# Sliding-window attention and a feed-forward pair on one core: dense 128-key segments in place of block-diagonal 64-key blocks

## The chip, the cores and the metric

The kernel runs on one core of a Trainium2 chip. The metric is the device time of one execution in microseconds (us). The engines are TensorE (PE in the profile, its weight loads PEld), VectorE (DVE), ScalarE (ACT), GpSimd (POOL) and SyncE (SP), which here only issues transfers. Each engine has its own queue of instructions and takes them in order; semaphores tie the queues together.

## What is computed

Eight batches of eight heads, 576 tokens, 64 elements a head. A query sees the keys at most 32 tokens away. The outputs of the heads, side by side, are the input of a feed-forward pair with a leaky ReLU between its layers. Inputs and output are 32-bit floats.

```python
B, H, S, D = q.shape                       # 8, 8, 576, 64
scores = (1 / sqrt(D)) * matmul(q, k.transpose(0, 1, 3, 2))
mask = abs(pos[:, None] - pos[None, :]) <= 32
attn = softmax(where(mask, scores, -1e9))
x = matmul(attn, v).transpose(0, 2, 1, 3).reshape(B * S, H * D)   # 4608 x 512
h = x @ w_in                               # 512 x 2048
out = maximum(0.01 * h, h) @ w_out         # 2048 x 512
```

## The kernel before

**Work units.** Heads go in pairs `p` (four pairs), batches in halves `hf` of 288 tokens. One attention *step* `i` is one pair in one half: 64 steps, `i // 8` the batch, `i // 4 % 2` the half, `i % 4` the pair (`where`, L267). Four steps fill the 288 columns of `xT` that one *group* `g` of the feed-forward needs: 16 `h` tiles of four matmuls each (`h_tile`, L360; matmul L348, ACT's leaky ReLU into `gT` L355), then output tiles `o` of 128 tokens, 16 matmuls each (`o_tile`, L381; L390, ACT's copy L395, SP's store L396), two or three to a group.

**Getting q and k transposed.** `load_qk` (L68) brings a pair's q and k into `qf`, `kf`. `cast_qk` (L186) makes them bf16 in `qb`, `kb`, which have a place for each of the four pairs. For batches 0 and 1 `transposes` (L218) turns them on TensorE and ACT copies them out. From batch 2 on (`BY_DMA = 2`) `transpose_dma` (L207) issues two transposing DMAs a pair on SP, one for q, one for k, and the rows come two tokens at a time (512 bytes), so that tokens lie even ones first. `place_keys` (L248) then has DVE copy the keys of the two heads into the two diagonal blocks of `kbd`: 64 keys of one head and 64 of the other in one 128 x 128 weight tile, zero elsewhere. `vbd` holds the values likewise (`cast_v`, L199). So one matmul serves both heads.

**A step.** `score(i)` (L270): five matmuls, one per 64-key block (`WIN`, L141), 544 columns in all, into `ps`; ACT's exponential into `e` (L280); POOL's product with the 0/1 mask into `prob` (L282). `join` (L287): DVE adds the two halves of `prob`. `sums` (L295): a matmul with block-diagonal ones (L301; two matmuls, L304, in the first twelve steps, which have no `join`) gives every row its head's sum in `s`, and DVE takes the reciprocal `r` (L309). `product` (L312): five matmuls with `vbd` into `x` (L320). `scaled` (L332): DVE writes `x * r` into `xT` (L334).

**Order.** The order on each engine is that of the program text (`manual_schedule`). `step()` (L420) runs: `join(i + 1)`, `score(i + 2)`, then `sums(i)`, `product(i)`, `scaled(i)`, then `place_keys`, then what is due in this step: casts and transposes for a pair of the next batch with the loads of the batch after it, or a cast of v and its next load. The transposes of batch `b` and pair `p` are due at step 8(b-1) + p + 2 (one earlier for batch 2), their placing at step 8(b-1) + 4 + p. The opening (L461 to L566: steps 0 to 8's score) is written out by hand: there `sums(i + 1)` stands ahead of `product(i + 1)`, so that a reciprocal runs early. After it a plan (L571 to L588) gives `h` tiles 0.49 us and quarter `o` tiles 0.86 us and spreads the steps between them; the last step of a group is due `LEAD = 4.0` us of the plan before the group's first `h` tile. `spend` (L592) runs what is due between tiles. `ps`, `s` and `x` have one buffer each, the `h` and `o` tiles four (`mmps`).

Of the kernel before, what the change touches and what calls it, by code (L numbers as in the profile page):

```python
# [16 lines left out]
def kernel(  # L17
# [9 lines left out]

    nc = tc.nc
# [8 lines left out]
    NB = S // 64  # L41
    HALF = S // 2
    DMC = DMODEL // 128
    FFC = DFF // 128
    EVEN = HALF // 2
# [5 lines left out]
    cast = ctx.enter_context(tc.tile_pool(name="cast", bufs=1))  # L51
    attn = ctx.enter_context(tc.tile_pool(name="attn", bufs=2))
    kt = ctx.enter_context(tc.tile_pool(name="kt", bufs=4))
    joined = ctx.enter_context(tc.tile_pool(name="joined", bufs=2))
    recip = ctx.enter_context(tc.tile_pool(name="recip", bufs=3))
# [6 lines left out]

    qf, kf, vf = {}, {}, {}
    RUN = S // 96

    BY_DMA = 2

    def load_qk(b, p, behind=None):  # L68

        for into, src, name in ((qf, q, "qf"), (kf, k, "kf")):
            t = fload.tile([96, 2, RUN * D], FP32, name=f"{name}{p}")
            if behind is not None:
                behind.memset(t[0:1, 0, 0:1], 0.0)
                behind = None
            heads = src[b, 2 * p:2 * p + 2]
            if b < BY_DMA:
                nc.sync.dma_start(out=t, in_=heads.rearrange("a (p c) d -> p a (c d)", c=RUN))  # L79
            else:  # L80
                nc.sync.dma_start(
                    out=t.rearrange("p a (g e) -> p a g e", g=3),
                    in_=heads.rearrange("a (g p c) d -> p a g (c d)", g=3, c=2),
                )
            into[b, p] = t

    def load_v(b, p):

        t = fload.tile([128, NB, D], FP32, name=f"vf{p}")
        for a in range(2):  # L90
            nc.sync.dma_start(  # L91
                out=t[64 * a:64 * a + 64],
                in_=v[b, 2 * p + a].rearrange("(c p) d -> p c d", p=64),
            )
        vf[b, p] = t
# [9 lines left out]

    ident_f = const.tile([128, 128], FP32)
# [4 lines left out]
    ones_bd = const.tile([128, 128], BF16)  # L111
    nc.vector.memset(ones_bd, 0.0)
    nc.vector.memset(ones_bd[0:64, 0:64], 1.0)
    nc.vector.memset(ones_bd[64:128, 64:128], 1.0)


    qb = const.tile([96, NPAIR, RUN, 2, D], BF16)
    kb = const.tile([96, NPAIR, RUN, 2, D], BF16)

    kbd = [const.tile([128, NPAIR, NB, 128], BF16, name=f"kbd{i}") for i in range(2)]  # L120
    vbd = [const.tile([128, NPAIR, NB, 128], BF16, name=f"vbd{i}") for i in range(2)]
    zero = const.tile([128, 1], BF16)
    nc.vector.memset(zero, 0.0)

    def clear(t, p):
        flat = t[:, p].rearrange("p n j -> p (n j)")
        nc.scalar.activation(
            out=flat, in_=zero.to_broadcast([128, NB * 128]), func=AF.Copy,
        )

    mask = [const.tile([128, 2, 2, EVEN], BF16, name=f"mask{i}") for i in range(2)]
    nc.vector.memset(mask[0][:, 1, :, 0:16], 0.0)
    nc.vector.memset(mask[1][:, 1, :, 128:EVEN], 0.0)
    nc.vector.memset(kbd[0], 0.0)
    clear(vbd[0], 0)
    clear(vbd[0], 1)
    clear(vbd[0], 2)

    WIN = [  # L141
        [((0, 0, 48), (2, 48, 64), (4, 112, 32)), ((1, 16, 64), (3, 80, 64))],
        [((4, 0, 32), (6, 32, 64), (8, 96, 48)), ((5, 0, 64), (7, 64, 64))],
    ]

    win = const.tile([128, 2, 3, 64], BF16)
    nc.gpsimd.memset(win, 1.0)
    for lo in (0, 64):
        w = win[lo:lo + 64]
        nc.gpsimd.affine_select(  # L150
            out=w, in_=w, compare_op=ALU.is_ge, fill=0.0,
            base=0, channel_multiplier=-1, pattern=[[1, 2], [0, 3], [2, 64]],
# [3 lines left out]
            base=2 * W, channel_multiplier=1, pattern=[[-1, 2], [0, 3], [-2, 64]],  # L156
        )
    nc.gpsimd.memset(vbd[0][:, 3], 0.0)
    win_f = win.rearrange("p c m i -> p c (m i)")

    def make_mask(hf):
        lo = (16, 32)[hf]
        nc.gpsimd.tensor_copy(out=mask[hf][:, 0], in_=win_f[:, :, lo:lo + EVEN])
        lo = (16, 0)[hf]
        nc.gpsimd.tensor_copy(out=mask[hf][:, 1, :, lo:lo + 128], in_=win_f[:, :, 0:128])

    NPROB = 6
    prob = const.tile([128, NPROB, 2, 2, EVEN], BF16)

    ps = scps.tile([128, 1024], FP32)  # L170
    P0 = 512 - HALF
    ps_v = ps[:, P0:P0 + 2 * HALF].rearrange("p (n c i) -> p n c i", n=2, c=2)
    nc.scalar.activation(
        out=ps[:, 512:512 + HALF], in_=zero.to_broadcast([128, HALF]), func=AF.Copy,
    )

# [7 lines left out]
    qT = {}  # L184

    def cast_qk(b, p, q_eng=None):  # L186
        for eng, src, dst in ((q_eng or nc.gpsimd, qf, qb), (nc.gpsimd, kf, kb)):
            if b < BY_DMA:
                parts = [(dst[:, p], src[b, p].rearrange("p a (c d) -> p c a d", d=D))]
            else:  # L190
                by_c = src[b, p].rearrange("p a (g c d) -> c p g a d", g=3, c=2)
                parts = [(dst[:, p, 3 * c:3 * c + 3], by_c[c]) for c in range(2)]
            for to, tok in parts:
# [142 lines left out]
    def weighted(i):  # L336
        if probs[i][2] is None:
            sums(i)
# [308 lines left out]
```

## Time and profile before

| what | value |
|---|---|
| runs | 318.67, 318.82, 319.0 us; median 318.82 us |
| profiled execution, its span | 318.5 us, 6474 instructions; the three runs lie 0.2 to 0.5 us above the span, and the page has no other time for this execution |
| granted TensorE clock | 1.000 |
| DMA | 49.46 MB in 108400 packets, mean 155 GB/s; SP's queue 66.8% of 16 engines, POOL's 8.0% |
| DMA landing, median | q 4.5, k 5.0, v 4.2, transposes 4.1 (q) and 3.2 us (k) |
| idle before POOL's mask | 87.8 us over 64 |

The span is cut into 40 slices of 8 us on the page; a digit is the busy share of an engine in a slice, in tenths. A row of the groups has the line, the engine, the operation, the tiles and shapes, the count, the busy time of the group, the mean length of one in ns, and the engine's idle time just before them with what ended it. The chain of waits is followed from the last instruction back to what released it; its pieces have start, length and work. `SPq` means the queue of SP: its rows are the issues of DMAs, and their length is the time that SP spends on issuing.

### The profile page before, as it was taken

To read this page: it belongs to the slowest core of one execution; us is meant where nothing else is said; L and a number is where in the kernel's file an instruction comes from. 1 tells how busy PE (TensorE), PEld (TensorE's weight loads), DVE (VectorE), ACT (ScalarE), POOL (GpSimd) and SP (SyncE) were. 2 spreads that over 40 slices of the span, in tenths; PEclk is the share of its full clock that TensorE was granted. 3 is DMA by queue.
4 is the path that set the end of the run, shared out by engine and by line. 5 is a ranking of instruction groups with operands and counts; after the bars stand their busy time and mean duration, and the time that the engine had idled before them with its cause. 6 is when DMAs were issued, how large, how long until landed. Compare 5 with 4: busy or idle time off the path is not lost.

```text
span 318.5 us, 6474 instructions
## 1 busy us (share of the span) xinstructions
PE 303.2 (95%) x2449; PEld 204.3 (64%) x2449; DVE 218.2 (69%) x259; ACT 182.6 (57%) x393; POOL 191.6 (60%) x251
## 2 busy tenths in 40 slices
PE   2679998999999999999999999999999999999996
PEld 1467774585765858576765858576665858576653
DVE  5678955869655997688755997688745988565100
ACT  7577698474652828374652828375552837464531
POOL 7798963974546866686546866586637866330000
PEclk9999999999999999999999999999999999999999
DMA  8999999997999995399735995399733430000101
GB/s 179 211 186 218 267 250 203 250 206 181 216 242 196 231 206 150 82 251 203 155 76 127 238 227 136 75 223 232 162 76 104 109 70 33 35 35 2 66 31 71
DMA packets 108400, 49.46 MB, mean 155 GB/s; under 512 B 68816, under 2 KB 103888, under 8 KB 108368
## 3 DMA queue, kind: packets, MB, share of 16 engines
q1 hardware_dynamic: 104144, 44.84, 66.8%
q0 software_dynamic: 4224, 4.19, 8.0%
q8 instruction: 19, 0.31, 0.4%
q14 instruction: 13, 0.11, 0.1%
HBM read 36.70 MB, written 9.44 MB: 145 GB/s over the span
## 4 chain that ended last, share of the span: by engine, by line
PE 89%; DMA 3%; DVE 2%; SPq 1%; POOL 1%; ACT 1%; issue 1%; DVEq 0%; ACTq 0%
PE mm L348 39%; PE mm L390 38%; PE x L320 5%; PE ps L275 4%; DMA kf<-in_k_dram 3%; PE s L301 2%; DVE r L309 2%; SPq L79 1%; POOL w_in_bf L448 1%; DVE xT L334 1%; PE tp L225 1%; PE s L304 1%; ACT vbd L203 0%; SPq L91 0%; POOL prob L282 0%
## 5 line engine op out<-in xcount | busy, mean ns | idle before, releaser
L309 DVE RECIPROCAL r<-s 128x288 f32<-128x288 f32 x64 | 125.2, 1956 | 56.5 <-PE s L301 53.3
L282 POOL TENSOR_TENSOR prob<-e,mask 128x576 bf16<-128x576 bf16 x64 | 81.5, 1274 | 87.8 <-ACT e L280 41.1
L348 PE MATMUL mm<-xT,w_in_bf 128*128 128x288 bf16 x1024 | 134.0, 286 | 0.3
L390 PE MATMUL mm<-w_out_bf,gT 128*128 128x512 bf16 (+2 forms) x592 | 130.4, 373 | 0.2 <-DMA w_out_bf<-in_moe_w_out_dram 0.2
L355 ACT ACTIVATE gT<-mm 128x288 bf16<-128x288 f32 x256 | 101.4, 412 | 24.8 <-PE mm L348 8.5
L348 PEld LDWEIGHTS <-w_in_bf 128*128 128x128 bf16 x1024 | 98.4, 98 | 24.8 <-issue 0.6
L390 PEld LDWEIGHTS <-gT 128*128 128x128 bf16 x592 | 56.3, 98 | 59.6 <-issue 0.3
L395 ACT ACTIVATE o_sb<-mm 128x512 f32<-128x512 f32 (+2 forms) x37 | 21.7, 586 | 92.0 <-PE mm L390 92.0
L280 ACT ACTIVATE e<-ps 128x576 bf16<-128x576 f32 x64 | 41.4, 648 | 9.4 <-PE ps L275 9.2
L197 POOL CAST kb<-kf 96x384 bf16<-96x384 f32 (+1 forms) x56 | 35.5, 656 | 4.6 <-DMA kf<-in_k_dram 4.6
L205 POOL CAST vbd<-vf 64x576 bf16<-64x576 f32 x50 | 34.5, 689 | 1.8 <-DMA vf<-in_v_dram 0.4
L334 DVE TENSOR_TENSOR xT<-x,r 128x288 bf16<-128x288 f32 x64 | 29.3, 458 | 8.2 <-PE x L320 1.2
L260 DVE COPY kbd<-kT 64x576 bf16<-64x576 bf16 x48 | 32.3, 672 | 0.3
L275 PE MATMUL ps<-qT,kbd 128*128 128x128 bf16 (+2 forms) x320 | 26.5, 215 | 1.8 <-DVE kbd L258 1.2
L275 PEld LDWEIGHTS <-kbd 128*128 128x128 bf16 x320 | 21.0, 100 | 10.6 <-DVE kbd L258 1.5
L320 PE MATMUL x<-prob,vbd 128*128 128x128 bf16 (+2 forms) x320 | 26.0, 213 | 1.3 <-ACT vbd L203 0.7
L197 POOL CAST qb<-qf 96x384 bf16<-96x384 f32 x48 | 24.5, 538 | 0.0
L320 PEld LDWEIGHTS <-vbd 128*128 128x128 bf16 x320 | 20.6, 99 | 3.9 <-ACT vbd L203 1.8
L292 DVE TENSOR_TENSOR both<-prob 128x288 bf16<-128x288 bf16 x52 | 19.7, 380 | 0.9
L301 PE MATMUL s<-both,ones_bd 128*128 128x288 bf16 x52 | 14.9, 286 | 0.0
L258 DVE COPY kbd<-kT 64x576 bf16<-64x576 bf16 x16 | 7.1, 444 | 8.7 <-ACT kT L239 8.6
L225 PE MATMUL tp<-ident,qb 96*128 96x96 bf16 x48 | 4.4, 243 | 6.2 <-DVE qb L197 6.2
(43 smaller groups left out, 86.6 us busy)
## 6 DMA issues: line engine op xcount, KB each, us to landing
qf<-in_q_dram SPq DMA_DIRECT2D x32, 288.0 KB, 4.5
kf<-in_k_dram SPq DMA_DIRECT2D x32, 288.0 KB, 5.0
vf<-in_v_dram SPq DMA_DIRECT2D x64, 144.0 KB, 4.2
out_dram<-o_sb SPq DMA_DIRECT2D x35, 256.0 KB, 3.6
w_in_bf<-in_moe_w_in_dram POOLq DMA_DIRECT2D x4, 512.0 KB, 8.6
w_out_bf<-in_moe_w_out_dram POOLq DMA_DIRECT2D x4, 512.0 KB, 16.8
qT<-qb SPq DMA_TRANSPOSE x24, 4.1
kT<-kb SPq DMA_TRANSPOSE x24, 3.2
```

Source lines behind the costliest of these rows:

```text
L197: eng.tensor_copy(out=to, in_=tok)
L205: nc.gpsimd.tensor_copy(out=vbd[b % 2][r, p, :, r], in_=vf[b, p][r])
L260: nc.vector.tensor_copy(out=to.rearrange("p n (m c) -> p n c m", c=2), in_=kT[r].rearrange("p (c n m) -> p n c m", c=2, n=NB),)
L275: nc.tensor.matmul(ps_v[:, n_, :, i0:i0 + n], kbd[b % 2][:, p, blk], by_c[:, :, hf * EVEN + i0:hf * EVEN + i0 + n], start=True, stop=True,)
L280: nc.scalar.activation(out=e, in_=ps[:, P0:P0 + 2 * HALF], func=AF.Exp, scale=scale)
L282: nc.gpsimd.tensor_mul(pr.rearrange("p n c i -> p (n c i)"), e, mask[hf].rearrange("p n c i -> p (n c i)"),)
L309: nc.vector.reciprocal(r, s)
L320: nc.tensor.matmul(x_v[:, :, i0:i0 + n], vbd[b % 2][:, p, blk, :], pr[:, n_, :, i0:i0 + n], start=(blk == parts[0][1]), stop=(blk == parts ...
L334: nc.vector.tensor_mul(place(i), x, r)
L348: nc.tensor.matmul(h[:, 0:HALF], w_in_bf[:, c, ts(f, 128)], xT[:, c, ds(g * HALF % RING, HALF)], start=(c == 0), stop=(c == DMC - 1),)
L355: nc.scalar.activation(out=gT[:, f, ds(g * HALF % RING, HALF)].rearrange("p (i c) -> p i c", c=2), in_=h[:, 0:HALF].rearrange("p (c i) -> ...
L390: nc.tensor.matmul(o[:, lo:hi], gT[:, f, ds(128 * j % RING, 128)], w_out_bf[:, f, lo:hi], start=(f == 0), stop=(f == FFC - 1),)
```

## The change

The block-diagonal tiles go. A weight tile for the scores is now 128 keys of *both* heads' transposed rows: 128 consecutive columns of `kT` (64 elements of each head on 128 partitions). The queries are kept twice, `qz[.., a, ..]` having the rows of head `a` and zeros in the other head's 64 partitions, so that the contraction over 128 partitions yields one head's scores. Eight segments of 128 keys, 64 apart (`SEG`), serve 96, 64, 64, 64 and again 64, 64, 64, 96 queries. For odd segments `kO` holds the two 64-key halves exchanged (`swap`, one copy a pair), so that each row of `v` serves both kinds of segment from the partition it was loaded into. The weight tile of the products is `[values of head 0 | ones | values of head 1]`, of which 128 columns are taken: for head 0 rows 0 to 63 of the result are weighted sums of values and rows 64 to 127 are row sums, for head 1 the other way round. So there are two results, `x0` and `x1` (one buffer each), no matmul for sums, no `join`; instead two copies bring the sums to the partitions of their head, and the reciprocal stands between product and multiply. Tokens keep their natural order.

What moves or changes in number, per pair or step:

- q and k loads from batch 2 on: four DMAs of 256-byte rows in place of two of 512-byte rows; v: three DMAs in place of two.
- transposing DMAs: three (q twice) in place of two, into buffers that stay for a batch; the bf16 sources have two places (`p % 2`) instead of four.
- casts: q on POOL is one instruction in place of two, and so is k; v three in place of two.
- DVE: `swap` (one copy) in place of two copies into `kbd`, due at the same step; two multiplies of 64 partitions in place of one of 128; one or two copies of sums (the other one on ACT).
- the opening is written anew; in it the masks of the first two steps are multiplied on DVE, the q casts of pairs 2 and 3 are on POOL, and the clearing on DVE is of `qz` and the ones in `vw`.
- `LEAD` is 5.0.

The diff, cut to its core:

```diff
     def load_qk(b, p, behind=None):
...
             else:
-                nc.sync.dma_start(
-                    out=t.rearrange("p a (g e) -> p a g e", g=3),
-                    in_=heads.rearrange("a (g p c) d -> p a g (c d)", g=3, c=2),
-                )
+                for a in range(2):
+                    nc.sync.dma_start(out=t[:, a], in_=heads[a].rearrange("(g p) d -> p g d", p=96))
...
     def load_v(b, p):
...
+        t = fload.tile([128, 2, 5, D], FP32, name=f"vf{p}")
         for a in range(2):
             nc.sync.dma_start(
+                out=t[:, a, 0:4], in_=v[b, 2 * p + a, 0:512].rearrange("(j p) d -> p j d", p=128),
             )
+        nc.sync.dma_start(
+            out=t[0:64, :, 4], in_=v[b, 2 * p:2 * p + 2, 512:S].rearrange("a p d -> p a d"),
+        )
...
+    zero_halves(nc.vector, 0)
+    nc.vector.memset(vw[0][:, :, :, 1], 1.0)
...
+    def cast_v(b, p, engs=None):
...
+        copy(e0, to[:, 0], src[:, 0:4])
+        copy(e1, to[0:64, 1], src[0:64, 1:5])
+        copy(e2, to[64:128, 1], src[64:128, 0:4])
...
     def transpose_dma(b, p):
+        for a in range(2):
+            nc.sync.dma_start_transpose(
+                out=qz[b % 2][:, p, a].rearrange("p (c i) -> p c i", c=RUN),
+                in_=qbz[p % NQZ][:, a].rearrange("p c a d -> p (c a d)"),
+            )
+        nc.sync.dma_start_transpose(
+            out=kT[b % 2][:, p].rearrange("p (c i) -> p c i", c=RUN),
+            in_=kb[:, p % NQB].rearrange("p c a d -> p (c a d)"),
+        )
+        landing.append((8 * (b - 1) + 4 + p, b, p))
...
+    def transposes(b, p, engs):
...
+            if which == "q":
+                for a in range(2):
+                    r = slice(64 * a, 64 * a + 64)
+                    copy(engs[a], qz[b % 2][r, p, a].rearrange("p (i c) -> p i c", c=RUN), tok[r])
             else:
+                copy(engs[2], kT[b % 2][:, p].rearrange("p (i c) -> p i c", c=RUN), tok)
+                swap(b, p, engs[3])
...
+    def score(i, mask_eng=None):
         b, hf, p = where(i)
+        for n in range(hf * HSEG, (hf + 1) * HSEG):
...
+            nc.tensor.matmul(
+                ps[:, P0[hf] + c0:P0[hf] + c1].rearrange("p (a i) -> p a i", a=2), kk,
+                qz[b % 2][:, p, :, SEG[n][0]:SEG[n][1]], start=True, stop=True,
+            )
...
+    def product(i):
...
+        for a in range(2):
+            for n in range(hf * HSEG, (hf + 1) * HSEG):
...
                 nc.tensor.matmul(
+                    x[a][:, SEG[n][0] - first:SEG[n][1] - first],
+                    vw[b % 2][:, p, n, a:a + 2].rearrange("p c d -> p (c d)"),
+                    pr[:, c0 + a * w:c0 + (a + 1) * w],
+                    start=True, stop=True,
                 )
...
+    def normalize(i, engs):
...
+        copy(engs[0], s[0:64], x[0][64:128])
+        copy(engs[1], s[64:128], x[1][0:64])
         r = recip.tile([128, HALF], FP32, name="r")
         nc.vector.reciprocal(r, s)
+        for a in range(2):
+            rows = slice(64 * a, 64 * a + 64)
+            nc.vector.tensor_mul(xT[rows, p, t0:t0 + HALF], x[a][rows], r[rows])
...
+    def step(engs, swap_eng):
         i = state["done"]
-        if JOINED - 1 <= i < NC - 1:
-            join(i + 1)
         if i < NC - 2:
             score(i + 2)
-        weighted(i)
-        place_keys()
+        product(i)
+        normalize(i, engs)
+        while landing and landing[0][0] <= i:
+            swap(*landing.pop(0)[1:], swap_eng)
...
+    cast_qk(0, 0, DVE)
+    make_mask(0, DVE)
+    transposes(0, 0, (ACT, ACT, ACT, DVE))
+    score(0, DVE)
+    cast_qk(0, 1, DVE)
+    transposes(0, 1, (ACT, ACT, ACT, DVE))
+    cast_v(0, 0)
+    score(1, DVE)
     product(0)
+    normalize(0, (ACT, ACT))
+    cast_qk(0, 2, POOL)
+    transposes(0, 2, (ACT, ACT, ACT, DVE))
+    keep_busy(ps, 768, 4)
+    score(2)
+    cast_qk(0, 3, POOL)
     load_w_in(0, 512)
+    keep_busy(ps, 768, 4)
+    cast_v(0, 1)
+    product(1)
+    normalize(1, (ACT, ACT))
     load_w_in(512, 1024)
+    transposes(0, 3, (ACT, ACT, ACT, DVE))
+    keep_busy(ps, 768, 8)
+    score(3)
     load_w_in(1024, 1536)
+    cast_v(0, 2, (POOL, ACT, ACT))
+    make_mask(1, POOL)
     h0 = h_first(0)
     h = next(h0)
+    product(2)
+    normalize(2, (ACT, ACT))
     keep_busy(h, HALF, 8)
+    score(4)
+    load_w_in(1536, 2048)
+    cast_v(0, 3, (POOL, ACT, ACT))
+    next(h0)
+    next(h0)
+    product(3)
+    normalize(3, (ACT, ACT))
...
     def second_half():
-
         i = state["done"]
-        weighted(i)
-        if i < 7:
-            sums(i + 1)
+        product(i)
+        normalize(i, (ACT, DVE))
         if i < 5:
             score(i + 3)
         state["done"] += 1
...
-    H_US, O_US, LEAD = 4 * (HALF / 2400 + 2.5e-3), 4 * 0.216, 4.0
+    H_US, O_US, LEAD = 4 * (HALF / 2400 + 2.5e-3), 4 * 0.216, 5.0
...
-            step()
+            step((DVE, DVE) if kind == "h" else (ACT, DVE), DVE)
```

## The prediction

> **What bounds the kernel now.** I read the busy shares, the chain of waits, the groups, then the timelines of SP and of the opening. From the page:
>
> ```profile
> PE 303.2 (95%) x2449; PEld 204.3 (64%) x2449; DVE 218.2 (69%) x259; ACT 182.6 (57%) x393; POOL 191.6 (60%) x251
> PE   2679998999999999999999999999999999999996
> PE 89%; DMA 3%; DVE 2%; SPq 1%; POOL 1%; ACT 1%; issue 1%; DVEq 0%; ACTq 0%
> ```
>
> TensorE is busy in all slices but the first few: its work is the time, and any wait placed before one of its matmuls is added to it. Its steady stretch, in the chain of waits (start, length, work):
>
> ```profile
> 191.88 3.43 PE mm L348 x28
> 195.31 0.24 PE ps L275 x5
> 195.55 0.12 PE s L301
> 195.68 0.24 PE x L320 x5
> 195.91 3.92 PE mm L348 x32
> ...
> 204.38 0.24 PE ps L275 x5
> ...
> 208.43 0.24 PE ps L275 x5
> ```
>
> An attention step costs 0.24 + 0.12 + 0.24 = 0.60 us of TensorE; steps stand 4.05 to 4.5 us apart, 17.15 us to a group of four. The other engines have only to keep this beat. How near they are to it:
>
> ```profile
> L309 DVE RECIPROCAL r<-s 128x288 f32<-128x288 f32 x64 | 125.2, 1956 | 56.5 <-PE s L301 53.3
> L334 DVE TENSOR_TENSOR xT<-x,r 128x288 bf16<-128x288 f32 x64 | 29.3, 458 | 8.2 <-PE x L320 1.2
> 131.10 1.25 SPq L212 DMA_TRANSPOSE qT<-qb  x1
> 132.44 1.20 SPq L212 DMA_TRANSPOSE kT<-kb  x1
> 133.70 0.57 SPq L81 DMA_DIRECT2D qf<-in_q_dram  x1
> 134.33 0.50 SPq L81 DMA_DIRECT2D kf<-in_k_dram  x1
> 134.92 0.45 SPq L396 DMA_DIRECT2D out_dram<-o_sb  x1
> 135.86 1.30 SPq L212 DMA_TRANSPOSE qT<-qb  x1
> ```
>
> (Two rows of the groups, six of SP's timeline.) SP spends 4.3 us of each step of this kind on issuing; the beat is 4.3.
>
> **TensorE's work.** Per matmul: 3.92/32 = 122.5 ns for 288 columns, 3.45/16 = 215.6 for 512, so 0.416 ns a column and 2.7 ns each; five of 544 columns make 0.240, as the rows show. New: four score matmuls with 576 columns 0.251, eight products with 576 columns 0.262, no sum: 0.51 us. Saved: 0.09 x 52 steps = 4.7 us; the first 12 steps lose a second sum matmul as well, but lie where TensorE will wait. Products of 64 columns at 29 ns each have a weight load per matmul; the old streams have one every 47 ns on average without a gap, which is the nearest row. Bounds: 29 ns holds (saving 4.7), or 47 ns is a floor (eight products 0.38: step 0.63, a loss of 1.6). I take 29.
>
> The Trainium skill, "TensorE: Matmul & The Clock Gate", section "Back-to-back issue gap", speaks against small matmuls: it gives some 81 ns for each 128-column matmul with its weight load; by it twelve instead of eleven would cost 0.08 us a step more. These rows deny it: five of 64 to 128 columns take 0.24 us, 48 each.
>
> **The opening** (the first four steps). Each engine runs in order, so I walk the compiled order with the row durations. DVE first clears two halves of qz and sets the ones: 4352 elements at 0.86 ns (the 2304-word memset took 1.98), 3.7 us against 2.4 of memsets now; its q cast starts at 5.65 (before 4.65). A pair then costs: q cast 1.0; 0.69 to ACT's first copy; three ACT copies (two halves of q, k) 0.60 apart, the last 0.65; swap 0.44 (L258's row); 0.75 from score to exponential; exponential 0.65; mask on DVE 0.6 (between 0.38, the 288-column add, and POOL's 1.27): 6.1. And DVE's q cast of pair 1 is queued *behind* mask 0, so pair 1's mask ends at 17.8. Then reciprocal 0 (1.96) and two 64-partition multiplies (0.46 each, starts 0.37 apart) to 20.7; swap 2 is queued behind them; score 2, exponential to 22.5; POOL's mask 2 (1.27) to 23.8, and *behind it* both casts of pair 3 (2 x 1.0), a w_in issue (0.8) and three v casts of pair 1 (0.6 each, from the 64x576 row of 0.69): 28.2. Only there can product 1 run. Two ACT copies of the sums, reciprocal, multiplies 32.2; swap 3, score 3, mask 3 35.3; w_in, v cast: product 2 at 36.8. Mask for half 1, mask 4, w_in, v cast: product 3 at 41.4; its normalization ends 45.5. So the fourth chunk of the first hidden tiles starts at 45.5, not where the chain has it now:
>
> ```profile
> 25.88 0.47 DVE xT L334
> 26.39 0.65 PE mm L348 x4
> 64.33 1.47 PE mm L348 x12
> ```
>
> That is **+19.2 us**. DMA no longer gates it: the last k load lands at 15.5. Bounds: a third of the links at half price, +12; TensorE running cold in its gaps (its six opening transposes take 0.66, later 0.42), +23.
>
> **Steps 4 to 7.** Old: s and x are separate, the reciprocal runs before the product, and a step waits 0.46 for one multiply. New: x0 and x1 have one buffer each and hold from product to multiply: 0.3 drain, copy 0.41, reciprocal 1.96, multiplies 0.83, some 0.1 at each of four handovers, ACT's queue of gT (0.41 each) and exponentials ahead of the copy: 3.7 to 4.4 us. The program gives 16 matmuls (1.96 us) between these steps. Walked: products at 47.3, 51.9, 55.8, 59.6 and group 1's fourth chunk done at 64.3, that is 17.0 us from product 4; now 28.15 to 36.95, 8.8. **+8.2** (6 to 10).
>
> **Steps 8 to 11** stand 12, 12 and 8 output matmuls apart (2.59, 2.59, 1.73 us plus 0.51). With four chains of 4.45 they take 17.8, now 51.06 to 64.33, 13.3; ahead of them some 1.9 of old waits go. **+2.6** (0 to 4).
>
> **The steady steps, x held.** Gaps from product to product become 3.95 or 4.45 us. x1 is free 4.07 us after the product with both copies on DVE, 4.2 to 4.4 with one on ACT behind the exponential and an o_sb copy (0.60), and is wanted at gap + 0.13. So a stall of 0 to 0.35 in half the steps: 0.25 a group, **+3** (0 to 8). DVE loses the add (0.38) and two key copies a pair (2 x 0.67) and gains copies, a second multiply and the swap: 3.3 to 3.7 a step plus 0.44 in half of them, against 4.2 (now 3.5 on average). No cover is left, so whatever DVE waits for stops TensorE.
>
> **SP's queue, and what waits for it.** Per pair of batches 3 to 6, SP now issues three transposes (1.30 from start to start, 3.9), four q/k loads with as many pieces each as the old two (0.59, 2.35) and 0.3 of output: 6.55 us, at a step of 4.2. The lag grows by 2.35 a pair, 7.05 at the fourth. Step start T; its casts end T+3.4; the fourth pair's k transpose is issued at 3.45 + 3 x 6.55 + 2.6 = 25.7 and lands 3.2 later, 28.9 (landing times 2.5 to 4.9). Its swap, an instruction of DVE, stands at T + 5 x 4.2 + 4.3 = 25.3; behind it on DVE are the next step's copies, reciprocal and multiplies, for which the next product's x waits. 3.6 us late a batch, four batches 14.4; batch 3 inherits up to 3 from batch 2 (whose transposes share SP with the v loads), and the x stalls give back about 1 a batch: **+14**. Bounds: 0, if the issues of 256-byte rows cost half; 22, if landing takes the 4.9 of the slowest. Batches 2 and 7 are in time: an extra step, or no loads. POOL's q cast is one instruction for two; its v casts three for two, +0.4 a step in half the steps, hidden by its idle time, 87.8 us over 64 masks; were it not, the mask still has two steps of lead. ACT's contiguous gT costs nothing either way: its strided rows of 288 and the plain ones of 512 columns (0.41, 0.59) lie on one line per column.
>
> **Sum**: 318.5 (span) - 4.7 + 19.2 + 8.2 + 2.6 + 3 + 14 = 360.8. The median of the three runs, 318.82, lies 0.3 above the profiled span: **361 us**.
>
> **Rivals.**
> A (0.57): the above, 351 to 373.
> B (0.20): SP is not late, since a swap finds its keys landed; the stalls of opening and x stay: 361 - 14 = 347, 342 to 351. For it: SP now idles up to 1.7 us a pair for POOL's casts. Against: the fourth burst's transpose follows the loads without a gap.
> C (0.09): the opening overlaps more than I walk, +10 instead of +19 and the groups behind it half: 318.8 - 4.7 + 10 + 5.4 + 3 + 3 = 335, 325 to 342.
> D (0.05), faster: TensorE's own work decides. If x is free before the next product, everywhere less than the gap (the chain under 2.5 us in group 0, that is, no reciprocal in it), the saved matmuls remain: 318.8 - 4.7 - 1.5 = 312.6. The 89% of the chain speaks for it; the reciprocal of 1.96 between product and multiply against.
> E (0.08): over 373: SP's lag carries over from batch to batch (4 x 6.55 and 4 x 1.9 for three v loads a pair, 33.8 us of issue, against 33.6 of beat) and loads come late too: 380.
> That it does nothing: 0.01; the order of every engine differs.
>
> The range leaves out D, E and the lower half of C: 334 to 373. The likeliest case's own range is 351 to 373. A change under 0.2% could not be told from none: faster 0.05, same 0.01, slower 0.94.
>
> **What would show it.** In the profile after: first slices of TensorE at 2 to 5 tenths until about 60 us; the h matmuls of the fourth chunk first starting near 45; product matmuls (x) idle before, released by DVE's multiply; DVE's swap idle before, released by the DMA of kT, in the last two pairs of batches 3 to 6; SP nearly without idle in those batches. Wrong if product 1 runs before 22 us, if SP's q/k issues take under 0.4 us, or if steady steps stand at 4.2 us throughout.

## The result and the profile after

The changed kernel takes **373.47 us** (median of four runs, 372.72 to 374.59) against 318.91 us for the kernel before in the same session (318.67 to 319.82): a ratio of 1.171, with a 95% interval of 1.168 to 1.173. Its profiled execution has a span of 372.2 us, 53.7 more than the 318.5 of before. The forecast was 361 us, with a range up to 373, so the measured time lies just above the range: direction and places are as walked, the size is 12.5 us short. In two experiments below one of four runs is a slow one, at a lower granted clock (358.62 us in loads later without the reciprocal, 370.13 us in both edits with the v loads on ACT); the medians given hold it, the ratios leave it out.

Of the page after, the busy shares, TensorE's slices (9.3 us each), the granted clock in the same slices, and the chain that ended last:

```profile
PE 314.0 (84%) x2504; PEld 205.2 (55%) x2504; DVE 249.5 (67%) x335; ACT 195.2 (52%) x427; POOL 194.7 (52%) x243
PE   1513686987999997689996999879998999999996
PEclk9999997899999999899999899989999999999999
PE 56%; DVE 16%; DMA 10%; POOL 6%; issue 6%; ACT 4%; SPq 2%; POOLq 0%; DVEq 0%; ACTq 0%
```

TensorE's first six slices stand at 1 to 8 tenths, and its row of nines is now broken in several later places. The chain is 56% TensorE where it was 89%; what came in is DVE (16%) and DMA (10%).

The two groups of DVE that were shown of before (work, shapes, count, then busy time and mean ns, then idle time and what ended most of it):

```profile
L287 DVE RECIPROCAL r<-s 128x288 f32<-128x288 f32 x64 | 125.0, 1953 | 27.0 <-ACT s L180 25.0
L290 DVE TENSOR_TENSOR xT<-x,r 64x288 bf16<-64x288 f32 x128 | 58.3, 455 | 4.5
```

The reciprocal costs what it did, but its idle time halved (56.5 to 27.0) and now ends with ACT's copy of the sums, no longer with a matmul; the multiplies doubled in number at almost the same length (455 ns, 458 before). In all DVE is busy for 249.5 us, 218.2 before.

The opening, in the chain of waits (start, length, work):

```profile
28.49 0.35 PE x L271 x3
...
29.73 1.96 DVE r L287
...
37.15 0.66 PE x L271 x8
...
42.74 0.43 PE x L271 x4
...
65.49 0.47 DVE xT L290
65.96 0.04 issue
66.00 1.12 PE mm L298 x4
```

Products 1, 2 and 3 stand within 1.4 us of where the prediction's walk through the queues put them (28.2, 36.8, 41.4), each behind POOL's v cast; product 1 is followed by two sums, the reciprocal and two multiplies. The last row is the fourth chunk of group 1, behind DVE's multiply; it ends near 66.5, before near 36.95.

SP in batch 3 (start, length, what is issued):

```profile
129.58 1.05 SPq L78 DMA_DIRECT2D vf<-in_v_dram  x2
130.68 0.61 SPq L81 DMA_DIRECT2D vf<-in_v_dram  x1
131.38 1.10 SPq L78 DMA_DIRECT2D vf<-in_v_dram  x2
132.53 0.61 SPq L81 DMA_DIRECT2D vf<-in_v_dram  x1
133.24 2.54 SPq L203 DMA_TRANSPOSE qz<-qbz  x2
135.88 1.22 SPq L207 DMA_TRANSPOSE kT<-kb  x1
137.15 1.14 SPq L71 DMA_DIRECT2D qf<-in_q_dram  x2
138.33 1.05 SPq L71 DMA_DIRECT2D kf<-in_k_dram  x2
139.48 0.52 SPq L340 DMA_DIRECT2D out_dram<-o_sb  x1
140.10 2.56 SPq L203 DMA_TRANSPOSE qz<-qbz  x2
```

SP has no pause beyond the 0.05 to 0.1 us between issues. From pair to pair (133.24 to 140.10) SP needs 6.86 us, where a step should take 4.2 to 4.5. The first transposes of the batch stand behind v loads, although their casts are done at 127.5; the last of them in POOL's rows:

```profile
126.64 0.83 POOL L182 CAST kb<-kf 96x768 bf16<-96x768 f32 x1
```

DVE some us later, in its timeline (start, length, work; in brackets idle time before it and what ended it):

```profile
146.28 2.54 DVE L182 COPY kO<-kT 128x512 bf16<-128x512 bf16 x1 [3.68 <-DMA kT<-kb]
148.75 0.93 DVE L182 COPY s<-x 64x288 f32<-64x288 f32 x2
149.72 1.95 DVE L287 RECIPROCAL r<-s 128x288 f32<-128x288 f32 x1
151.70 0.94 DVE L290 TENSOR_TENSOR xT<-x,r 64x288 bf16<-64x288 f32 x2
```

The waits of the whole span in which this shows (total us, times, longest):

```profile
DVE kO L182 <- DMA kT<-kb: 20.3, 10, 4.4
PE x L271 <- POOL vw L182: 15.6, 6, 3.8
PE x L271 <- DVE xT L290: 13.9, 12, 3.1
```

Four of the six waits put down to POOL's v cast (10.0 us) are those of the opening. The other two, 2.82 and 2.77 us ahead of products 33 and 41, are late swaps as well: the first ends at 202.89, when POOL's cast had been done since 199.27; DVE's first multiply, which frees x0, ends at 202.75.

And TensorE's timeline after it:

```profile
152.30 0.82 PE L271 MATMUL x<-prob,vw 128*128 128x64 bf16 x8 [3.08 <-DVE xT L290]
152.92 5.01 PE L334 MATMUL mm<-w_out_bf,gT 128*128 128x512 bf16 x16
```

Together they are the whole chain of a late swap: the copy kO waits 3.68 us for kT; behind it on DVE are the sums, the reciprocal and the multiplies; the next product stands 3.08 us, because x is still held. After the wait, 16 output matmuls took 5.01 us, and the granted clock was 0.50 from 152.4 to 155.7. The timeline of before has 3.62 for 16:

```profile
187.67 3.62 PE L390 MATMUL mm<-w_out_bf,gT 128*128 128x512 bf16 x16
```

**Where the 53.7 us of span are.** Up to the first h matmul of group 2 the kernel lost 32.7 us (97.02 against 64.33); from there to the end it took 275.2 us instead of 254.2, 21.0 more. For the second part I sorted TensorE's time by the distance from each matmul's start to the next: 0.416 ns a column and 2.7 ns is the work, a large excess is a gap, a small one a slow matmul. Work fell from 251.2 to 245.9; gaps rose from 0 to 20.9; slow matmuls from 0 to 5.3. Of the gaps, 17.3 us stand at the steps with a late swap, most of the rest comes 0.27 us at a time, x held.

### The profile page after: what moved, and what is told of

Same layout as the page of the kernel before. It is cut to its first block, busy times and chain, and to the rows that moved or that the text cites. A ratio compares the mean times of both kernels' runs of the same rounds, so it can differ in the third digit from the quotient of the medians.

```text
span 372.2 us, 6882 instructions
## 1 busy us (share of the span) xinstructions
PE 314.0 (84%) x2504; PEld 205.2 (55%) x2504; DVE 249.5 (67%) x335; ACT 195.2 (52%) x427; POOL 194.7 (52%) x243
## 4 chain that ended last, share of the span: by engine, by line
PE 56%; DVE 16%; DMA 10%; POOL 6%; issue 6%; ACT 4%; SPq 2%; POOLq 0%; DVEq 0%; ACTq 0%
PE mm L298 27%; PE mm L334 21%; DVE r L287 8%; PE x L271 4%; DVE xT L290 4%; DMA kT<-kb 3%; DMA vf<-in_v_dram 3%; PE ps L252 3%; DMA qf<-in_q_dram 2%; POOL prob L259 2%; DVE s L182 2%; POOL vw L182 2%; SPq L203 1%; ACT s L180 1%; DMA qz<-qbz 1%
## 5 line engine op out<-in xcount | busy, mean ns | idle before, releaser
L257 ACT ACTIVATE e<-ps 128x576 bf16<-128x576 f32 x64 | 41.6, 650 | 63.6 <-PE ps L252 59.0
L290 DVE TENSOR_TENSOR xT<-x,r 64x288 bf16<-64x288 f32 x128 | 58.3, 455 | 4.5
L271 PE MATMUL x<-prob,vw 128*128 128x64 bf16 (+1 forms) x512 | 33.7, 202 | 32.1 <-POOL vw L182 15.6
L182 DVE COPY s<-x 64x288 f32<-64x288 f32 x87 | 39.4, 453 | 31.9 <-PE x L271 30.3
L182 POOL CAST vw<-vf 64x512 bf16<-64x512 f32 (+1 forms) x88 | 52.4, 612 | 2.3 <-DMA vf<-in_v_dram 0.4
L271 PEld LDWEIGHTS <-vw 128*128 128x128 bf16 x512 | 24.8, 100 | 39.9 <-POOL vw L182 17.1
L182 POOL CAST kb<-kf 96x768 bf16<-96x768 f32 x32 | 27.8, 870 | 11.4 <-issue 6.4
L182 DVE COPY kO<-kT 128x512 bf16<-128x512 bf16 x32 | 14.2, 444 | 24.5 <-DMA kT<-kb 20.3
L252 PE MATMUL ps<-qz,kT 128*128 128x128 bf16 (+1 forms) x128 | 24.0, 236 | 5.6 <-ACT kT L180 5.6
L180 ACT ACTIVATE s<-x 64x288 f32<-64x288 f32 x41 | 16.7, 407 | 21.7 <-PE x L271 20.9
L252 PE MATMUL ps<-qz,kO 128*128 128x128 bf16 (+1 forms) x128 | 23.4, 236 | 4.2 <-DVE kO L182 4.1
L182 POOL CAST qbz<-qf 96x768 bf16<-96x768 f32 x24 | 19.6, 818 | 7.0 <-DMA qz<-qbz 7.0
```

The costliest lines, as they stand in the source:

```text
L180: eng.activation(out=to, in_=frm, func=AF.Copy)
L182: eng.tensor_copy(out=to, in_=frm)
L252: nc.tensor.matmul(ps[:, P0[hf] + c0:P0[hf] + c1].rearrange("p (a i) -> p a i", a=2), kk, qz[b % 2][:, p, :, SEG[n][0]:SEG[n][1]], start=T ...
L257: nc.scalar.activation(out=e, in_=ps[:, P0[hf]:P0[hf] + 2 * HALF], func=AF.Exp, scale=scale)
L271: nc.tensor.matmul(x[a][:, SEG[n][0] - first:SEG[n][1] - first], vw[b % 2][:, p, n, a:a + 2].rearrange("p c d -> p (c d)"), pr[:, c0 + a * ...
L290: nc.vector.tensor_mul(xT[rows, p, t0:t0 + HALF], x[a][rows], r[rows])
```

## The experiments

In what follows "loads later" and "opening" are the edits of the first two runs. Ratios are to the kernel before, with the 95% interval in brackets. The kernel before took 319.1 to 319.9 us beside them.

### Loads later

```
             transpose_dma(b, p)
-            if 2 < b < B - 1:
-                load_qk(b + 1, p)
...
             cast_v(b, p)
             if b + 1 < B:
                 load_v(b + 1, p)
+            if 2 < b < B - 1:
+                load_qk(b + 1, p)
```

> The q and k loads of batches 4 to 7 are issued four steps later than in the changed kernel, with the v loads; nothing else moves, the bytes and the number of DMAs are the same. Theory (SP's queue: in four steps of a batch it has 6.55 us of issuing per step of 4.2, so the keys' transposes, DVE's swap behind them and the next product come late): the waits of DVE's swap for kT fall from 20.3 us to under 8 (batch 3 keeps its own, which it has from batch 2), TensorE's stalls from group 2 on from 20.9 us to about 10 and its slow matmuls there from 5.3 to about 2: 373.5 - 14 = 359 us. Rival (the DMA engines are too full, whoever issues first, or the transposes themselves are slow): the waits stay, 370 to 375 us.

Measured: 358.19 us (357.86 to 358.53), ratio 1.120 [1.117, 1.124], as expected. No transfer, byte or instruction was taken away; the order on SP alone is worth 15.3 us. The wait of DVE for kT fell from 20.3 us to 3.2.

### Opening

```
     cast_qk(0, 0, DVE)
+    cast_qk(0, 1, DVE)
     make_mask(0, DVE)
     transposes(0, 0, (ACT, ACT, ACT, DVE))
     score(0, DVE)
-    cast_qk(0, 1, DVE)
...
     cast_qk(0, 2, POOL)
+    cast_qk(0, 3, POOL)
+    cast_v(0, 1)
     transposes(0, 2, (ACT, ACT, ACT, DVE))
...
     score(2)
-    cast_qk(0, 3, POOL)
     load_w_in(0, 512)
     keep_busy(ps, 768, 4)
-    cast_v(0, 1)
```

> Order alone, in the opening: DVE's q cast of pair 1 goes ahead of the masks, POOL's casts of pair 3 and of v of pair 1 go ahead of the third mask. Theory (the opening is a chain of in-order queues: a cast stands behind a mask whose exponential comes late): product 1 runs at about 21 us instead of 28.5, product 2 at about 30 instead of 37.2, the fourth chunk of the first hidden tiles at about 40 instead of 47.1; everything after it is shifted: 373.5 - 7.5 = 366 us. Rival (the opening waits for the loads or for the clearing, not for the order): under 2 us, 372 to 374.

Measured: 365.64 us, ratio 1.144 [1.140, 1.147]. Product 1 started at 20.6 us instead of 27.3, product 2 at 29.3 instead of 37.2. What was queued ahead of two casts and a mask was on the path, as the walk had it.

### No reciprocal

```
-        nc.vector.reciprocal(r, s)
+        nc.vector.tensor_copy(out=r, in_=s)
```

> Leaves out the reciprocal: a copy of s to r takes its place, so the output is not normalized. Everything else is as in the changed kernel. Theory (x0 and x1 are held over the chain copy, reciprocal, two multiplies, and this chain is longer than the gap to the next product): the chain falls by about 1.6 us; opening -6 us (four links), the stalls of steps 4 to 11 -10 us, those from group 2 on -8 us of which 3 are x stalls and 5 late swaps that then hurt less, slow matmuls -4 us: 345 us (338 to 352). Rival (the stalls are waits for keys and casts, and the chain is covered): 362 to 370 us.

Measured: 357.77 us, ratio 1.119 [1.116, 1.122]: between the two. TensorE came earlier to batch 3 (product 12 at 88.5 us, 96.6 with the reciprocal) and then waited longer. Its waits have

```profile
DVE kO L182 <- DMA kT<-kb: 40.5, 12, 5.4
```

twice the 20.3 us of the changed kernel. A part of the gain was handed to another wait.

### Filled gaps

```
+        if i in (33, 41):
+            fill()
         if i < NC - 2:
             score(i + 2)
+        if i == 23:
+            fill()
         product(i)
```

> Adds 12 matmuls of 320 columns (1.6 us) into an unused part of ps ahead of products 23, 33 and 41, where TensorE stalls for 3 us or more in the changed kernel; results are unchanged. Theory (after a stall of about 3 us TensorE runs at half its clock for some 3.4 us, which costs 1.7 us a time on top of the stall): the stalls shrink by what the fill takes, the slow matmuls behind them vanish: 373.5 - 5 = 368.5 us, granted clock from 0.977 to about 0.99. Rival (matmuls are slow there because of transfers or buffers, not for idling): 373 to 374 us, slow matmuls as before; if the fills hold up products: up to 376.

Measured: 373.16 us, ratio 1.167 [1.162, 1.172], the rival's number. The slow matmuls did go where filled: 28 h matmuls after product 33 took 3.59 us instead of 5.27. But later waits grew: the one before step 25 from 1.83 to 2.90 us, that of step 49 from 1.20 to 2.69 (from the start of one matmul to the next, less its work). Behind these two the matmuls were slow again: 32 h matmuls took 5.75 us and 28 took 5.27, at a granted clock of 0.50, and the mean clock of the run is 0.977 as in the changed kernel. So the fills moved the slow matmuls more than they removed them, and what was won at three places was lost at later waits. What the slow matmuls cost by themselves this run does not show.

### Both edits, and loads later without the reciprocal

> The two edits before together, in the changed kernel: the q/k loads of batches 4 to 7 issued four steps later, and, in the opening, DVE's cast of pair 1 ahead of the first mask and POOL's casts of pair 3 and v casts of pair 1 ahead of the second mask. If the opening and the SP queue are separate terms of one sum, the gains add: 373.5 - 15.3 - 7.8 = 350 us (348 to 353). Rival: a TensorE that comes earlier to batch 3 only waits longer there for SP, as it did without the reciprocal: 354 to 358.

Measured: 353.59 us, ratio 1.107 [1.105, 1.110]: the opening adds 4.6 of its 7.8 us, nearer to the rival (354 to 358) than to the sum of gains. It is the fastest version that leaves nothing out, and 34 us behind the kernel before.

> The q/k loads four steps later, and a plain copy in place of the reciprocal: the normalization is left out, the output holds products multiplied by the row sums instead of divided. Theory: without the reciprocal alone only 15.7 us went, since TensorE then waited 20 us more for SP's queue; with SP relieved, the chain from product to multiply shows its whole price, 7.5 (steps 4 to 7) + 4 (steps 8 to 11) + 6 (two normalizations of the opening at 1.5 each, on the path three times) + 3 (x held in the steady steps) + about 4 of stalls that remained: 358.2 - 22 = 336 us (331 to 340). Rival: what it gave before is all that it is worth, 358.2 - 15.7 = 342.5 (341 to 346).

Measured: 355.35 us (353.29 to 358.62), ratio 1.111 [1.105, 1.117]. **A miss**: 2.8 us, or 4.6 without the run of 358.62 (median then 353.61), where 22 were expected. TensorE was 8 us ahead after product 12, and had lost 6 of it by product 32 (190.4 against 192.3 us), with 10.0 us of gaps and 4.4 of slow matmuls between 130 and 200. Here SP issued the first transposes of batch 3 at 127.02, 8 us after their casts were done (119.0), behind the loads of q, k and v.

### The swap on POOL

```
-            step((DVE, DVE) if kind == "h" else (ACT, DVE), DVE)
+            step((DVE, DVE) if kind == "h" else (ACT, DVE), POOL)
```

> The changed kernel with one edit: from batch 2 on the swap of the transposed keys is done by POOL instead of DVE; SP's order is untouched. POOL's masks have two steps of lead, DVE's copies have none. Theory 1, that a late kT is dear only because the waiting swap stands ahead of DVE's copies and multiplies: the waits of DVE for kT go, POOL's wait is covered, 373.5 - 15 = 358 us (355 to 363). Theory 2, that SP is itself the pace of batches 3 to 6, so that removing one wait moves it to the next that SP feeds (the exponential's mask behind the swap, POOL's casts waiting for source buffers): 368 to 374.

Measured: 364.97 us, ratio 1.143 [1.141, 1.146]: 8.5 us, between the two. The wait moved to POOL and grew:

```profile
POOL kO L182 <- DMA kT<-kb: 34.1, 12, 4.9
```

So the swap's place on DVE is worth 8.5 us. That the masks' lead covers part of POOL's longer wait, and a late kT costs the rest wherever it is waited for, was not tried.

### SP's burden in the kernel before

In the loads of the kernel before, for b > 2, and in its transposes:

```
+            elif b > 2:
+                for a in range(2):
+                    nc.sync.dma_start(
+                        out=t[:, a].rearrange("p (g d) -> p g d", d=D),
+                        in_=heads[a].rearrange("(g p) d -> p g d", p=96),
+                    )
...
+        spare = kt.tile([128, S], BF16, name="spare")
-        for t, src in ((qT[b][:, p], qb), (kT, kb)):
+        for t, src in ((qT[b][:, p], qb), (spare, qb), (kT, kb)):
```

> The kernel before, with SP's burden of the changed kernel alone: from batch 3 on each pair's q and k are loaded by two transfers of 256-byte pieces in place of one of 512-byte pieces (keys and queries are then in another token order, so the output is not the reference's), and from batch 2 on a third transpose, of q into a spare tile, is issued between the other two. If SP's lag alone makes the term, whatever waits for it: +13 us, 332 (327 to 337). Rival, that the old kernel's DVE, with 0.7 us a step to spare and no swap, takes the lag up: 319 to 323.

Measured: 341.95 us, ratio 1.071 [1.067, 1.074]: +22.9 us, more than either theory. None of the new attention is in this kernel, no swap and no held x; its DVE now waits for kT at the key copies, which before did not wait for it at all:

```profile
DVE kbd L267 <- DMA kT<-kb: 31.7, 15, 4.1
```

The second edit alone:

> The kernel before with only the third transpose of each pair (of q into a spare tile, batches 2 to 7) added to SP, without the split loads; the output is the reference's. The two together cost 22.9 us. If the price starts where SP's issues of a pair no longer fit the step (4.3 us then, 5.6 now, 6.8 with both, at steps of 4.2 to 4.5), the half burden costs much less than half: +4, 323 us (320 to 327). Rival, that each DMA more costs its share: +11.5, 330 (328 to 333).

Measured: 334.08 us, ratio 1.044 [1.040, 1.049]: +14.5. My threshold was wrong: the third transpose alone costs more than half, the split loads the other 8. SP falls behind with it alone: the fourth pair's transposes of batches 4 to 6 are issued 3.9 to 5.0 us after the end of their casts, in the kernel before between 0.5 us ahead of it and 0.2 after. The transposes themselves are not slower: kT lands 2.6 us (median) after its issue in both runs of this section, 3.2 before.

### The v loads on ACT

```
+        dma = nc.scalar if b > 1 else nc.sync
         for a in range(2):
-            nc.sync.dma_start(
+            dma.dma_start(
```

and in a step the v loads of the step before are issued after its normalization.

> The changed kernel with one edit: the v loads of batches 2 to 7 on ACT's queue, one step later. It tells the two forms of the SP term apart. If SP's lag arises within each batch (transposes and q/k loads 6.55 us in a step of 4.2 to 4.5, and time to recover in the four steps with v loads alone), only what batch 3 inherits from the v loads of batches 2 and 3 goes: 373.5 - 5 = 368 us (366 to 371). If the lag carries over from batch to batch because SP's 34 us of issue fill the batch's 34 to 36 us, it goes with the v loads: 357 to 363.

> As the run with later q/k loads and a copy in place of the reciprocal (the normalization is left out), and the v loads of batches 2 to 7 are issued by ACT's queue, one step later than by SP. That run's SP stood at 93 to 95% of nearly every 20 us from 100 us on, and TensorE, 8 us ahead after the opening, stood again in batches 3 and 4 (10.0 us of gaps and 4.4 of slow matmuls between 130 and 200 us). Theory: SP's issuing had become the pace, so that a shorter opening and a shorter chain were given back; with 6.6 us of v issues a batch taken off SP, 355.35 - 15 = 340 us (336 to 344), which is then the price of the chain in full. Rival: the place of the loss is POOL's and DVE's own order, not SP's: 350 to 355.

> The changed kernel with later q/k loads, the reordered opening and the v loads of batches 2 to 7 on ACT's queue; its output is the reference's. Theory (SP is the pace after a shorter opening): of the 353.6 us without the last edit go the gaps of batch 3 (5.5 and 1.7 of slow matmuls between 130 and 200 us) less the 1 to 2 us of held x in them, 353.6 - 5.5 = 348 us (345 to 350). Rival: 352 to 355, or over it if ACT's new issues (6.6 us a batch on an engine that is 52% busy) delay its exponentials and sums.

Measured: 386.26 us, 373.71 us and 367.69 us, that is 12.8, 18.4 (20.1 against 353.61) and 14.1 us *slower* than the same kernels with these loads on SP. **Three misses**, since the edit brought a wait of its own. ACT's timeline in the first of them:

```profile
162.06 0.98 ACTq L79 DMA_DIRECT2D vf<-in_v_dram  x2
163.08 0.72 ACTq L82 DMA_DIRECT2D vf<-in_v_dram  x1
163.85 0.60 ACT L340 ACTIVATE o_sb<-mm 128x512 f32<-128x512 f32 x1 [4.01 <-issue]
```

ACT's output copy stands 4.01 us behind the issue of loads into a buffer that POOL is casting from only at 160.76 to 162.59, and TensorE waits 4.20 us for that copy. The reading is from the rows; it was not tried further. The first run still tells where the lag arises: its SP issues the first transposes of batch 3 in time (at 133.52, as soon as the first of their two casts is done), and yet those of the fourth pair come 6.7 us after their casts; DVE's wait for kT stayed at 20.4 us (20.3 with the loads on SP). The lag arises within the batch.

### Loads left out

To take the loads out of SP's queue without putting them elsewhere, the next four kernels reuse what lies in the buffers:

```
             if b + 1 < B:
-                load_v(b + 1, p)
+                vf[b + 1, p] = vf[b, p]
...
             if 2 < b < B - 1:
-                load_qk(b + 1, p)
+                qf[b + 1, p], kf[b + 1, p] = qf[b, p], kf[b, p]
```

The first line alone in the first two runs (in the first together with loads later and no reciprocal), both lines in the last two.

> As the run with later q/k loads and a copy in place of the reciprocal, and the v loads of batches 3 to 7 are left out: each takes the values of batch 2 that lie in its buffer (so neither values nor normalization are the reference's). Nothing is put on another engine. Theory: SP's queue took back what the shorter chain gave, so 355.35 - 15 = 340 us (335 to 345), and batch 3's first transposes are issued within 2 us of their casts instead of 8. Rival: 350 to 355, the loss then has another place.

> The changed kernel without the v loads of batches 3 to 7 (batch 2's values are used again, so the output of batches 3 to 7 is not the reference's). Theory, a lag within each batch: SP's 6.8 us a pair at steps of 4.2 to 4.5 are untouched, only the 5.8 us by which batch 3's first transposes follow their casts go: 373.5 - 5 = 368.5 us (365 to 371). Rival, a lag carried from batch to batch because all issues of a batch hardly fit in it: 6.6 us of issue a batch less take it away, 355 to 362.

> The changed kernel without the v loads of batches 3 to 7 and without the q/k loads of batches 4 to 7: their casts take the data of batch 2 and 3 again (the output of batches 3 to 7 is not the reference's). SP then issues transposes and output alone from batch 4 on, 3.9 + 0.6 us a pair. Theory: all 17.3 us of gaps before late swaps go, and with them 3.5 of slow matmuls: 373.5 - 20.8 = 353 us (350 to 356). Rival: the transposes' own 3.9 us a pair and their landing keep part of the wait, 358 to 366.

> The run before together with the reordered opening (same parts left out). Theory: with SP's queue empty the opening's 7.8 us add in full, 353 - 7.8 = 345 us (342 to 348), where with the loads in place they added only 4.6 of them. Rival: 348 to 353.

Measured: 339.74 us (ratio 1.063 [1.061, 1.065]), 368.14 us (1.149 [1.143, 1.155]), 352.49 us (1.103 [1.101, 1.105]) and 344.78 us (1.078 [1.077, 1.080]), each within 0.6 us of the number that the SP theory gave. In the first, SP is in time; its rows, and POOL's of the same stretch:

```profile
119.03 1.10 SPq L71 DMA_DIRECT2D kf<-in_k_dram  x2
120.24 3.06 SPq L203 DMA_TRANSPOSE qz<-qbz  x2
123.40 1.22 SPq L207 DMA_TRANSPOSE kT<-kb  x1
```

```profile
117.55 0.90 POOL L182 CAST qbz<-qf 96x768 bf16<-96x768 f32 x1
118.40 0.82 POOL L182 CAST kb<-kf 96x768 bf16<-96x768 f32 x1
```

The casts end at 119.2, the transposes start at 120.2, one us later instead of eight. So the 15.6 us (13.9 against 353.61) missing in the run without reciprocal had gone to SP's queue. In the third, DVE's wait for kT is gone from the waits altogether. These kernels also move fewer bytes, but that is not what brings kT in time: it lands 2.6 us (median) after its issue in the changed kernel, with later loads and without the loads alike.

## Why the prediction had the places right and SP's term too small

Predicted and measured terms, in us of span; the measured ones add up to the 55 us between the span before and the median after:

| term | predicted | measured | from |
|---|---|---|---|
| opening, to the fourth chunk | +19.2 | +20.7 | 47.12 against 26.39 |
| steps 4 to 7 | +8.2 | +8.8 | 66.5 against 36.95 at their end: 29.5, less 20.7 |
| steps 8 to 11 | +2.6 | +3.2 | 97.0 against 64.33: 32.7, less 29.5 |
| TensorE's work, from there | -4.7 | -5.3 | 245.9 against 251.2 |
| x held and what remains | +3 | +4.4 | without loads the rest is 350.4 - 97.0 = 253.4, before 254.2: -0.8, less -5.3 |
| SP's queue | +14 | +21.8 | spans 372.2 and 350.4, with and without the loads |
| median over span | +0.3 | +1.3 | 373.47 - 372.2 |

**TensorE's work: right.** Eight products with 64 to 96 columns take the 0.26 us computed, at 29 ns each of the small ones; there is no floor of 47 ns.

**The opening: right, and its cause shown for the larger part.** Products 1 to 3 came within 1.4 us of the walk. Moving the casts of three tiles took 7.8 of the 20.7 us back, so the order of DVE's and POOL's queues, not data, was the path; without the reciprocal product 4 comes 3.3 us earlier (46.9 for 50.2). The rest follows the walk and was not tried. TensorE did run slowly there (8 matmuls of 288 columns in 2.13 us at 38.94, in 1.14 at 58.28), but the bound of +23 built on that was not reached.

**Steps 4 to 11 and the held x: right within 0.6 and 1.4 us.** The chain from product to multiply is the cause as far as the reciprocal is concerned: from product 4 to product 12 the changed kernel takes 46.4 us, without the reciprocal 41.6, the kernel before 37.9. Product 12 then comes at 88.5 instead of 96.6 us, and with SP's queue relieved the kernel falls to 339.7. The other links of the chain were not taken apart.

**SP's queue: the step that failed, in its size: 14 us in the sum, 21.8 measured.** The mechanism stood: transposes and loads late, the swap waiting on DVE in batches 3 to 6, the next product behind it. Undone by leaving loads out it gives 21.0 us in the medians, of which the order of the loads alone gives 15.3; done by itself in the kernel before it costs 22.9.

The 14 were 3.6 us a batch in four batches, 3 more in batch 3, and less 1 a batch that the x stalls were to give back. On TensorE the gaps at late swaps are 17.3 us, which is the walked 14.4 + 3. What failed is the rest of the term. The x stalls gave back 0.8 us at most, not 4: the other gaps are 3.6 us, where 4.4 remain without the loads. And the slow matmuls after the waits, 5.3 us, stood in the sum at nothing. 17.3 - 0.8 + 5.3 are the 21.8.

That the gaps met the walk is in part luck, since its pieces were off on both sides. A pair was priced 6.55 us, the sum of issue rows; from pair to pair it is 6.86, 7.93 and 6.79 in batch 3, and 7.15 on average over batches 3 to 6. Gaps of 0.05 to 0.1 lie between all issues, the output takes 0.5, and single issues take longer (a transpose of k 2.33 instead of 1.22 us). Batch 3 inherits 5.8 us and not "up to 3": its first transposes are issued at 133.24, their casts done at 127.5. A late swap took up to 2.54 us instead of 0.29. On the other side kT landed 2.6 us after its issue, not 3.2. POOL's q casts of the third and fourth pair of batch 3 wait 7.0 us for the transposes of the pair two earlier, but SP's rows have no pause there, so this did not hold SP up. The upper bound of 22 lies near the measured term by luck: it was made for a landing of 4.9 us.

**Rival E, that the lag carries over from batch to batch**, would have been the other way to miss on this side. It fell: in batches 4 to 6 of the changed kernel the first transposes are issued in time again, as soon as the first of their casts is done, and the fourth pair's 6.3 to 8.1 us after their casts. The v loads taken off SP (run with loads left out, v alone) gave 5.3 us, about what batch 3 had inherited, and not 12 to 18; the order of loads within the batch gave 15.3. **Rival B**, SP not late, is the kernel without the loads: 352.5, not 347, since the opening and the small terms were each a little larger. **Rival C**, a shorter opening, fell with the 20.7 us. **Rival D** fell with the reciprocal between product and multiply, as argued against it.

**The slow matmuls** (5.3 us after the waits) had no term in the prediction. Filling three waits moved them behind two others and moved the total by 0.3 us, so how much of the 5.3 us a kernel without them would save stays open.

Three expectations of mine failed on the way for one reason: I added gains of edits that stand one behind the other. Without the reciprocal alone, with later loads besides, and with both edits, the earlier TensorE ran into SP's queue and part of the gain came back as waiting; once the queue was empty the opening's 7.8 us added in full (352.5 to 344.8).

What stays open: why ACT's loads cost 13 to 18 us is only read from rows; and how much of the 7.8 us between 14 and 21.8 each of SP's delays (longer pairs, what batch 3 inherits, the slow swap) makes by way of gaps and slow matmuls was not separated. None of the versions tried beats the kernel before.

## What to carry to other kernels

Count the issuing engine like a compute engine: add up, per step and with the gaps between them, all DMAs that one queue must issue, and compare with the beat; at 4.3 us of a 4.3 us step a third transpose has no place. Look next at what stands behind the instruction that waits for such a DMA: here an in-order copy on DVE turned a late key transpose into a stop of TensorE. And measure a gain with the next bottleneck taken away as well, since two edits on one path do not add.

## What the runs showed of the hardware

- DVE's copy kO takes 0.295 us (median of 32) and took up to 2.54. The longest lie beside POOL's work. POOL's rows at the longest, which began at 146.28 and ended at 148.82:

```profile
145.85 0.82 POOL L182 CAST qbz<-qf 96x768 bf16<-96x768 f32 x1 [5.15 <-DMA qz<-qbz]
146.62 0.82 POOL L182 CAST kb<-kf 96x768 bf16<-96x768 f32 x1
147.41 1.27 POOL L259 TENSOR_TENSOR prob<-e,mask 128x576 bf16<-128x576 bf16 x1
```

  POOL's third instruction ends at 148.68, the copy 0.14 later. Another copy, of 1.23 us at 273.34, ends 0.16 after the mask that POOL began at 273.14. The Trainium skill, "SBUF — State Buffer", section "Who interferes with whom", says that a DVE copy in one of its two-port modes and a POOL instruction exclude each other for a whole instruction; the rows agree, and show a copy held through three of POOL's instructions in a row. It was not tried by itself.

- After a wait of about 3 us TensorE ran slowly for some us: 28 h matmuls in 5.27 us after 2.82 us of waiting (granted clock 0.50 from 203.5 to 206.9), 3.59 with the wait filled. The Trainium skill, "TensorE: Matmul & The Clock Gate", section "Part 1: The HAM clock gate", gives an idle window of some 3.4 us, free-running, after which the clock halves; here shorter waits were enough, 2.77 to 3.08 us in the changed kernel and 2.52 and 2.73 in the run with filled gaps, while after 1.66 us, and in the run of both edits with the v loads on ACT after 2.59 and 2.78 us, the granted clock stayed at 1.00. So these runs show no sharp length. What it cost in the sum stays open.

- A load issued by ACT stands in ACT's order like any of its instructions (ACT's copy 4.01 us behind it in the rows above): with the three v loads a pair, which cost SP 1.65 us of issue, on ACT the total rose by 13 to 18 us. That ACT's wait for their buffer is the whole reason is read from the rows only.
